# Block-sparse attention and a gated long convolution on one core: keys copied straight into their slots, and later queries split in natural layout and placed by two DMA transposes

## Chip, cores and metric

The kernel runs on one core of a Trainium2 chip. The metric is the device time of one launch in microseconds, as the median of several runs. A separate profiled execution gives the trace; its span goes from its first to its last instruction.

## What is computed

Attention over 4 batches of 8 heads, 768 positions of 64 elements. A query sees its own block of 64 keys and the blocks whose mean key gives one of its three highest gate scores, never a later position. The result is the input of a second stage: a projection to three parts, a circular convolution of one of them along the sequence with a given filter, a product of the three, and an output projection.

```python
def _attn_ref(q, k, v):
    B, H, S, D = q.shape                       # 4, 8, 768, 64
    block, top_k = 64, 3
    k_rep = k.reshape(B, H, n_blocks, block, D).mean(axis=3)
    gate_scores = np.einsum('bhsd,bhnd->bhsn', q, k_rep)
    gate_scores = np.where(causal, gate_scores, -1000000000.0)
    top_idx = np.argsort(gate_scores, axis=-1)[..., -top_k:]
    ...                                        # mask: blocks in top_idx and the own block
    scores = scale * np.matmul(q, k.transpose(0, 1, 3, 2))
    mask = mask & (pos[:, None] >= pos[None, :])
    scores = np.where(mask, scores, -1000000000.0)
    ...                                        # softmax over keys
    return np.matmul(attn, v)

def _moe_ref(x, w_proj, filter_fft, w_out):    # x: heads side by side, 4 x 768 x 512
    proj = x @ w_proj
    x1, x2, x3 = proj[..., :D], proj[..., D:2 * D], proj[..., 2 * D:]
    X2 = np.fft.rfft(x2, n=S, axis=1)
    H = np.fft.rfft(filter_fft, n=S, axis=0)[None, :, :]
    x2_conv = np.fft.irfft(X2 * H, n=S, axis=1)
    return (x1 * x2_conv * x3) @ w_out
```

All inputs and the output are float32.

## The kernel before

**Pairs.** Two heads are worked on together, so there are 16 pairs, four per batch. `prep(g)` brings keys, queries and mask of pair g into the form that the scores need, `attn(g)` computes scores, exponentials and weighted values, and `hyena(b)` does the second stage for a batch once its four pairs are there. `filt()` transforms the filter once, at the start.

**Preparing a pair (`prep`).** Keys of both heads lie side by side in `kn` with the position on the partitions. TensorE transposes them in six float32 blocks (L342), so that a PSUM bank holds head 0 on partitions 0 to 63 and head 1 on 64 to 127. VectorE sums blocks of 64 for the key means (L345), ScalarE casts to float16 into `k2` (L350), and GpSimd splits the means into a high and a low half, `km` (L363, L364). Queries go the same way (L374), but ScalarE scales and casts them into `q2h` (L377) and VectorE writes the rounding error into `q2l` (L380): the gate scores need more than float16 gives. A shuffle then moves each head from its 64 partitions of `k2` or `q2h` to partitions 0 to 63 of the slots `kt` and `qt` (L393 as a DMA from SP; for the first two pairs L395, on VectorE or GpSimd). Twenty small matmuls give the gate scores (L409); VectorE finds the third highest for every query (L422 to L428) and marks the blocks below it in `nm` (L434, L439); five transposes (L450) turn the marks, and two copies (L458) put them on partitions 64 to 75 of `qt`.

**Scores.** Partitions 64 to 75 of `kt` hold a constant, -30720 in the row of the key's block and 0 elsewhere (`eblk`), so that one matmul over 76 partitions (L480) gives score plus mask. ScalarE takes the exponential (L486), GpSimd clears what lies above the diagonal (L491), TensorE multiplies with the values (L508), and VectorE divides (L517, L521) into `xn`. A transposing DMA makes `xT` of it (L540); sums and differences of its halves (L546) go through matmuls with cosines and sines (L558, L565) into `XT`.

**Second stage.** L667 and L676 to L686 multiply in the frequency domain, L703 to L712 project the two other parts and multiply them, L730 transforms back, L761 is the output projection.

**Order.** There is no loop that runs in program order. `build` makes a list of operations, each with the engines that can do it, a cost and a due time `vt` in units of a pair; `plan` simulates five engines (TensorE, ScalarE, VectorE, GpSimd and SP, which issues every DMA), buffers and PSUM banks, takes at each step the operation that can start first, the more urgent first, and so writes out one order for all. `PAR` holds the numbers of the due times, `POOLS` the count of buffers. Each engine then works in that order, and a waiting instruction holds up all behind it on its engine or, on SP, in its queue. Until the planner's `warm_until` TensorE is fed with filler matmuls (L856) where it has nothing else. Operations with `lock` are planned so that VectorE and GpSimd don't overlap.

Of the kernel before, what the change touches and what calls it, by code (L numbers as in the profile page):

```python
# [9 lines left out]
FP32 = mybir.dt.float32  # L10
# [14 lines left out]
KR = D + NB  # L25
# [16 lines left out]
for _pi, _segs in enumerate(PIECES):  # L42
# [6 lines left out]
    p0=-2.579, p1=0.077, a0=0.0, pvlag=0.294, dlag=1.997, dlen=0.945, h0=5.459, hlen=3.658, f0=0.196,  # L49
    f1=4.432, ld=-1.443, s2a=-0.205, s2b=0.422, x0=0.488, x1=0.938, c0=0.578, c1=0.847, o0=1.481,  # L50
    o1=1.0, pen_dve=0.221, ahead=2.229, delta=0.029, queue=6.554, direct=2, late=2.0, w0=1.031, wl=1.656,
    wlag=-0.256, warm_until=30, tr0=-7.197, trl=1.834, fill0=0.703,
)

POOLS = dict(kn=3, qn=3, vn=2, k2=2, q2h=2, q2l=2, ks=2, km=3, m8=2, nm=2,
# [8 lines left out]
class Buf:  # L64
    def __init__(self, pool):
        self.pool, self.slot, self.left = pool, None, 0
        self.w, self.r = {}, {}
        self.free = self.busy = 0.0
        self.users = []
# [7 lines left out]
class Graph:  # L77
    def __init__(self):
        self.ops = []

    def add(self, tag, vt, eng, emit, rd=(), wr=(), res=(), lock=False, size=0):
        o = Op()
        o.i, o.tag, o.vt, o.eng, o.emit, o.lock, o.size = len(self.ops), tag, vt, eng, emit, lock, size
# [25 lines left out]
def pe_cost(mms):  # L109
    occ = sum(mms)  # L110
    return occ, occ - mms[-1] + 0.17 + mms[-1]


def dve(n, rate=1.0):
    occ = n / (960.0 * rate) + 0.066
    return occ, occ + 0.15
# [11 lines left out]
def build(par):  # L128
    g_ = Graph()
# [56 lines left out]
    add("phase", T0, {"DVE": (1.0, 1.15)}, e_phase, wr=[cb("phase"), cb("magic")])  # L186
    add("iota", T0 + .1, {"POOL": pol(1.7)}, e_iota, wr=[cb("cols")])
    add("nyq", T0 + .2, {"DVE": (0.08, 0.23)}, e_nyq, wr=[cb("cols")])
    def e_eblk(E, nc, en):
        nc.gpsimd.memset(E.eblk[64:KR, :], EMASK)  # L190
        nc.gpsimd.affine_select(out=E.eblk[64:KR, :], in_=E.eblk[64:KR, :], compare_op=ALU.is_ge,
                                fill=0.0, base=0, pattern=[[1, S]], channel_multiplier=-64)
        nc.gpsimd.affine_select(out=E.eblk[64:KR, :], in_=E.eblk[64:KR, :], compare_op=ALU.is_ge,
                                fill=0.0, base=63, pattern=[[-1, S]], channel_multiplier=64)

    add("eblk", T0 + 3, {"POOL": pol(2.5)}, e_eblk, wr=[cb("eblk")])


    slot_init = []
    for i in range(POOLS["kt"]):  # L200
        def e_fill(E, nc, en, i=i):
            eng = nc.vector if en == "DVE" else nc.gpsimd
            eng.memset(E.t["qt"][i][64:KR, :, 0:P], 0.0)
            eng.tensor_copy(
                E.t["kt"][i][64:KR, :, :],
# [855 lines left out]
```

## Time and profile before

| | |
|---|---|
| time, median of 3 runs | 249.28 us (249.26 to 249.3) |
| span of the profiled execution | 248.8 us |
| TensorE matmuls, busy | 236.4 us (95%), 2410 of them |
| VectorE, busy | 204.8 us (82%) |
| ScalarE, busy | 175.6 us (71%) |
| GpSimd, busy | 129.3 us (52%) |
| DMA traffic | 40.02 MB, 98945 packets, 89440 of them under 512 B |
| mean granted TensorE clock | 0.991 |

The busy share is a mean over the whole span, in which stages follow one another that have different limits. Matmuls overlap in the record, so TensorE's busy time isn't the time that its work needs; the distance from one start to the next says more. Each digit of the following slices is the busy share of 6.2 us in tenths.

```profile
PE   8978998999889899999999999999999999999994
DVE  7899788988997999998899786778898968589860
ACT  2877999999667679886865796767756873524443
DMA  6999499997999958999976895421415131032006
```

### The profile page before, as it was taken

Reading aid. Unit: us, or ns where it says so; the run is one execution under the profiler, and the core shown is the slowest. Engines: PE = TensorE matmul, PEld = TensorE weight load, DVE = VectorE, ACT = ScalarE, POOL = GpSimd, SP = SyncE. Lnnn points to the kernel's source line nnn. Section 1 sums busy time; section 2 is a strip of 40 time slices with the busy share of each in tenths; the row PEclk is TensorE's granted clock in tenths of the full one; section 3 lists DMA queues with packets and bytes.
Section 4 is the critical chain, followed back from the end, with each engine's and each line's share of the span. In section 5 each row is a group of like instructions: output and inputs, shape, how many; then the busy total and the mean of one; then the engine's idle time right before and its main releaser. Section 6 shows DMA issues by size and latency. Waiting matters only on the chain.

```text
span 248.8 us, 6695 instructions
## 1 busy us (share of the span) xinstructions
PE 236.4 (95%) x2410; PEld 161.1 (65%) x2410; DVE 204.8 (82%) x643; ACT 175.6 (71%) x296; POOL 129.3 (52%) x240
## 2 busy tenths in 40 slices
PE   8978998999889899999999999999999999999994
PEld 6756687678556576867766677677566766645651
DVE  7899788988997999998899786778898968589860
ACT  2877999999667679886865796767756873524443
POOL 6662457675485547554558476643444614063420
PEclk9999999999997999999999999999999999999999
DMA  6999499997999958999976895421415131032006
GB/s 167 336 229 249 102 248 221 233 245 174 275 212 224 234 151 203 247 180 214 216 188 172 195 279 115 107 54 33 108 42 161 42 34 32 9 139 109 3 20 234
DMA packets 98945, 40.02 MB, mean 161 GB/s; under 512 B 89440, under 2 KB 93024, under 8 KB 98912
## 3 DMA queue, kind: packets, MB, share of 16 engines
q1 hardware_dynamic: 98912, 39.60, 66.3%
q8 instruction: 19, 0.31, 0.5%
q14 instruction: 14, 0.11, 0.2%
HBM read 24.64 MB, written 6.29 MB: 124 GB/s over the span
## 4 chain that ended last, share of the span: by engine, by line
PE 79%; DVE 7%; SPq 6%; DMA 3%; ACT 2%; issue 1%; DVEq 0%; ACTq 0%
PE ps L703 16%; PE ps L480 14%; PE ps L761 8%; PE ps L667 8%; PE ps L508 7%; PE ps L730 6%; PE ps L558 4%; SPq L274 3%; PE ps L374 3%; PE ps L342 3%; PE ps L409 2%; PE ps L450 2%; PE ps L565 2%; SPq L297 2%; DMA t<-in_moe_w_out_dram 2%; DVE t L676 2%
## 5 line engine op out<-in xcount | busy, mean ns | idle before, releaser
L486 ACT ACTIVATE ex<-ps 128x1024 f16<-128x1024 f32 (+1 forms) x96 | 86.1, 930 | 14.7 <-PE ps L480 14.4
L491 POOL TENSOR_SCALAR_AFFINE_SELECT ex<-ex 128x256 f16<-128x256 f16 x96 | 41.7, 437 | 52.4 <-ACT ex L486 51.6
L480 PE MATMUL ps<-qt,kt 76*128 76x512 f16 (+3 forms) x256 | 51.2, 310 | 0.3 <-ACT ex L486 0.3
L703 PE MATMUL ps<-xT,wp 128*128 128x384 f16 x256 | 50.5, 326 | 0.0
L703 PEld LDWEIGHTS <-wp 128*128 128x128 f16 x256 | 24.0, 97 | 14.1 <-issue 0.2
L686 POOL TENSOR_TENSOR Y<-t,t 128x512 f16<-128x512 f32 (+1 forms) x18 | 23.4, 1306 | 18.7 <-DVE t L676 18.3
L480 PEld LDWEIGHTS <-kt 76*128 76x128 f16 x256 | 23.1, 99 | 15.1 <-issue 1.4
L508 PEld LDWEIGHTS <-ex 128*128 128x128 f16 x672 | 25.2, 97 | 3.9 <-POOL km L363 0.4
L508 PE MATMUL ps<-va,ex 128*128 128x65 f16 x672 | 26.8, 193 | 0.2 <-DVE nm L434 0.2
L765 ACT COPY osb<-ps 128x512 f32<-128x512 f32 x24 | 14.2, 590 | 15.1 <-PE ps L761 15.0
L667 PE MATMUL ps<-wp,XT 128*128 128x512 f16 x96 | 23.7, 381 | 0.2 <-DVE t L676 0.2
L761 PE MATMUL ps<-wo,yT 128*128 128x512 f16 x96 | 23.8, 379 | 0.0
L751 POOL TENSOR_TENSOR yT<-prod,sd 128x384 f16<-128x384 f32 x16 | 15.9, 1000 | 13.5 <-DVE sd L745 11.2
L712 DVE TENSOR_TENSOR prod<-ps,x 128x384 f32<-128x384 f32 x32 | 17.6, 552 | 6.5 <-PE ps L703 6.2
L350 ACT CAST k<-ps 128x384 f16<-128x384 f32 x32 | 14.7, 481 | 11.3 <-DVE colv L182 4.6
L676 DVE TENSOR_TENSOR t<-ps,HA 128x512 f32<-128x512 f32 x24 | 16.5, 686 | 6.3 <-PE ps L667 6.2
L730 PE MATMUL ps<-G,Y 128*128 128x384 f16 x96 | 20.8, 326 | 0.0
L709 ACT CAST x<-ps 128x384 f16<-128x384 f32 x29 | 14.0, 483 | 9.4 <-PE ps L703 4.6
L345 DVE TENSOR_REDUCE ks<-ps 128x6 f32<-128x384 f32 x32 | 17.1, 552 | 4.1 <-ACT k L350 2.0
L380 DVE SCALAR_TENSOR_TENSOR q2l<-ps,q2h 128x384 f16<-128x384 f32 x32 | 17.0, 551 | 2.3 <-ACT q2h L377 2.2
L521 DVE TENSOR_TENSOR xn<-ps,rec 128x384 f16<-128x384 f32 x32 | 17.8, 556 | 1.0
L745 DVE TENSOR_TENSOR sd<-ce,ps 128x384 f32<-128x384 f32 x32 | 16.3, 549 | 2.2 <-PE ps L730 1.5
(106 smaller groups left out, 435.0 us busy)
## 6 DMA issues: line engine op xcount, KB each, us to landing
kn<-in_k_dram SPq DMA_DIRECT2D x32, 192.0 KB, 3.6
qn<-in_q_dram SPq DMA_DIRECT2D x32, 192.0 KB, 3.6
vn<-in_v_dram SPq DMA_DIRECT2D x16, 384.0 KB, 4.3
out_dram<-osb SPq DMA_DIRECT2D x24, 256.0 KB, 2.0
t<-in_moe_w_proj_dram SPq DMA_DIRECT2D x12, 256.0 KB, 4.2
kt<-k SPq DMA_DIRECT2D x28, 96.0 KB, 3.0
qt<-q2h SPq DMA_DIRECT2D x28, 96.0 KB, 3.5
t<-in_moe_filter_fft_dram SPq DMA_DIRECT2D x6, 256.0 KB, 4.6
```

Of the source, the lines that this page charges most:

```text
L480: nc.tensor.matmul(o[:, col:col + w], lhsT=E.sb(Kt[g])[0:KR, t, P * kc:P * (kc + 1)], rhs=E.sb(Qt[g])[0:KR, t, q0:q0 + w], start=True, sto ...
L486: nc.scalar.activation(E.sb(ex)[:, 0:w], E.sp(sp)[:, 0:w], AF.Exp, scale=ESC)
L491: nc.gpsimd.affine_select(out=dv, in_=dv, compare_op=ALU.is_ge, fill=0.0, base=0, pattern=[[0, 2], [1, P]], channel_multiplier=-1)
L508: nc.tensor.matmul(o[:, 65 * c:65 * c + 65], lhsT=E.sb(exs[pi])[:, col:col + P], rhs=E.sb(va[g])[:, t, kc, :], start=(kc == 0), stop=(kc = ...
L521: nc.vector.tensor_tensor(E.sb(xn)[:, :, t, :], pov[:, :, 0:64], E.sb(rec).rearrange("p (c n) -> p c n", n=1) .to_broadcast([P, NQ, D]), o ...
L667: nc.tensor.matmul(E.bk(xa), lhsT=w, rhs=E.wp[:, j, Dm:2 * Dm], start=(j == 0), stop=(j == NP - 1))
L676: nc.vector.tensor_mul(E.sb(dst), E.bk(xa), m)
L686: (nc.vector if en == "DVE" else nc.gpsimd).tensor_tensor(E.sb(Y)[ro, n_, :], E.sb(x)[ri, :], E.sb(y)[ri, :], op=op)
L703: nc.tensor.matmul(E.bk(xq)[:, 0:HS], lhsT=E.wp[:, d2, 2 * Dm * m + P * dc:2 * Dm * m + P * (dc + 1)], rhs=E.sb(xT[gs[d2]])[:, cs], start= ...
L712: nc.vector.tensor_mul(E.sb(prod)[:, cs], E.bk(xq)[:, 0:HS], E.sb(x1))
L730: nc.tensor.matmul(E.bk(cv)[:, 0:HS], lhsT=E.sb(Y)[:, 3 * p_ + n_, P * dc:P * (dc + 1)], rhs=E.G[:, 3 * p_ + n_, :], start=(n_ == 0), stop ...
L761: nc.tensor.matmul(E.bk(op_), lhsT=E.sb(yT)[:, d2, P * c:P * (c + 1)], rhs=E.wo[:, d2, :], start=(d2 == 0), stop=(d2 == NP - 1))
```

## The change

**Keys.** With the heads on opposite partition halves of a slot, no shuffle is needed for keys. The slots `kt` and `qt` become [128, 6, 2, 128]: for every 128 positions first the columns of head 1, then those of head 0. Head 0 keeps its 64 partitions below and the mask on 64 to 75; head 1 has its data on 64 to 127, the mask on 0 to 11 and zeros between, and its scores are matmuls over 128 partitions. So each half of the key transposes is copied from PSUM into the slot by two instructions of 64 partitions, on ScalarE or VectorE, and the constants of a slot cover more partitions.

**Queries and mask, pairs 0 to 7.** As before, but the shuffle keeps partitions and writes 256 B pieces; the marks are transposed with 128 columns of weights.

**Queries and mask, pairs 8 to 15** (`tm=8`). No TensorE transposes. ScalarE or VectorE scales and casts the queries in natural layout into `qx` in blocks of 128 columns, VectorE writes the rounding error into the blocks between, a transposing DMA (T1, ten blocks of 128 columns) makes the gate's operand `qg` of both. After the gate VectorE writes the marks over the error's place in `qx`, next to the scaled queries, and a second transposing DMA (T2, twelve blocks) writes queries, zeros and mask into `qt` at once.

**Planner.** New values in `PAR`, an offset of the due time and a penalty for VectorE per kind of operation, other costs, slots `kt`, `qt` and `qx` taken in the order of the pairs, and other buffer counts.

```diff
-KR = D + NB
+XW = 2 * P * NQ + 64
+NMW = 64 * NQ
+KR = (76, 128)
...
-    p0=-2.579, p1=0.077, a0=0.0, pvlag=0.294, dlag=1.997, dlen=0.945, h0=5.459, hlen=3.658, f0=0.196,
-    f1=4.432, ld=-1.443, s2a=-0.205, s2b=0.422, x0=0.488, x1=0.938, c0=0.578, c1=0.847, o0=1.481,
-    o1=1.0, pen_dve=0.221, ahead=2.229, delta=0.029, queue=6.554, direct=2, late=2.0, w0=1.031, wl=1.656,
-    wlag=-0.256, warm_until=30, tr0=-7.197, trl=1.834, fill0=0.703,
+    p0=-2.503, p1=0.149, a0=0.0, pvlag=0.364, dlag=1.728, dlen=1.178, h0=5.163, hlen=3.776, f0=-0.278,
+    f1=4.952, ld=-1.045, s2a=-0.184, s2b=0.461, x0=0.517, x1=0.943, c0=0.51, c1=0.761, o0=1.574,
+    o1=1.0, pen_dve=-0.346, ahead=3.319, delta=0.028, queue=6.537, direct=2, tm=8, kin=16, late=2.0,
+    w0=1.334, wl=1.579, wlag=0.085, warm_until=31.758, tr0=-4.639, trl=2.112, fill0=-0.29, v_yT=0.58, v_sd=0.159,
...
-POOLS = dict(kn=3, qn=3, vn=2, k2=2, q2h=2, q2l=2, ks=2, km=3, m8=2, nm=2,
+POOLS = dict(kn=2, qn=3, vn=2, k2=1, qx=4, ks=2, km=3, m8=2, nm=1,
...
+    def e_eblk(E, nc, en, h=0):
+        x = E.eblk[64 * h:64 * h + 64, :]
+        nc.gpsimd.memset(x, EMASK)
...
+    for h in range(2):
+        add("eblk", T0 + 3 + h, {"POOL": pol(2.2)}, lambda E, nc, en, h=h: e_eblk(E, nc, en, h), wr=[(cb("eblk"), h)])
...
-            eng.memset(E.t["qt"][i][64:KR, :, 0:P], 0.0)
-            eng.tensor_copy(
-                E.t["kt"][i][64:KR, :, :],
-                E.eblk[64:KR, :].rearrange("p (o s) -> p o s", o=1).to_broadcast([NB, 2, S]))
...
+            eng.memset(E.t["qt"][i][0:64, :, 0, :], 0.0)
+            eng.memset(E.t["qt"][i][64:76, 0, 1, :], 0.0)
...
+            for h in range(2):
+                r = slice(0, 64) if h == 0 else slice(64, 76)
+                eng.tensor_copy(E.t["kt"][i][r, :, h, :], E.eblk[r, :].rearrange("p (c s) -> p c s", s=P))
...
+                    nc.sync.dma_start(E.sb(dst)[:, :, 1 - t if src == "q" and g >= par["tm"] else t, :],
...
+        direct, by_dma, in_place = g < par["direct"], g >= par["tm"], g < par["kin"]
...
-                    nc.vector.tensor_copy(E.sb(k2)[:, cs], E.bk(kp)[:, 0:HS])
...
             add("kT", v(.0 + .1 * hf), {"PE": pe_cost([0.109] * 3)}, e_kt, rd=[(kn[g], 0), (kn[g], 1), cb("id32")], wr=[kp],
-                res=[k2, ks])
...
+            if in_place:
+                for t in range(2):
+                    def e_k2(E, nc, en, hf=hf, kp=kp, t=t):
+                        r = slice(64 * t, 64 * t + 64)
+                        (nc.scalar.copy if en == "ACT" else nc.vector.tensor_copy)(
+                            E.sb(Kt[g])[r, HC * hf:HC * (hf + 1), 1 - t, :],
+                            E.bk(kp)[r, 0:HS].rearrange("p (c s) -> p c s", s=P))
+                    add("k2", v(.05 + .1 * hf + .02 * t), {"ACT": act(HS), "DVE": dve(HS)} , e_k2, rd=[kp],
+                        wr=[(Kt[g], ("h", t, hf))])
...
+                u = 1 - t if by_dma else t
+                ru = slice(64 * u, 64 * u + 64)
+                cc = slice(12 * u, 12 * u + 12)
+                nc.gpsimd.tensor_copy(x[r, 2, 0:12], E.sb(ks)[r, :])
+                nc.gpsimd.tensor_tensor(x[ru, 1, cc], E.sb(ks)[r, :], x[r, 2, 0:12], op=ALU.subtract)
+                nc.gpsimd.tensor_copy(x[ru, 0, cc], x[r, 2, 0:12])
...
-                    o, i_ = E.sb(dst)[0:64, t, :], E.sb(src)[64 * t:64 * t + 64, :]
+                    r = slice(64 * t, 64 * t + 64)
+                    o = E.sb(dst)[r, :, 1 - t, :]
+                    i_ = E.sb(src)[r, col:col + S].rearrange("p (c s) -> p c s", s=P)
...
+                add(tag, vt, eng, e_sh, rd=[(src, 0), (src, 1)], wr=[(dst, ("h", t, 0)), (dst, ("h", t, 1))],
+                    size=0 if direct else 130, lock=direct)
...
+        if not in_place:
+            shuffle(k2, 0, Kt[g], v(.3), "shK")
...
+        if not by_dma:
+            for hf in range(2):
...
+                    nc.vector.scalar_tensor_tensor(out=E.sb(qx)[:, cl], in0=E.bk(qp)[:, 0:HS], scalar=QS,
...
+            shuffle(qx, 0, Qt[g], v(.4), "shQ")
...
+        else:
+            def blocks(E, first, c0):
+                x = E.sb(qx)
+                return bass.AP(tensor=x.tensor, offset=x.offset + first + 256 * c0, ap=[[XW, P], [256, NQ - c0], [1, P]])
...
+            def e_pq(E, nc, en):
+                eng = nc.vector if en == "DVE" else nc.gpsimd
+                eng.memset(E.sb(qx)[:, 0:64], 0.0)
+                eng.memset(E.sb(qx)[:, 192:320], 0.0)
...
+            def e_qh(E, nc, en):
+                i_ = E.sb(qn[g]).rearrange("p c t d -> p c (t d)")
+                if en == "ACT":
+                    nc.scalar.activation(blocks(E, 64, 0), i_, AF.Copy, bias=0.0, scale=QS)
+                else:
+                    nc.vector.tensor_scalar_mul(blocks(E, 64, 0), i_, QS)
...
+            def e_ql(E, nc, en):
+                nc.vector.scalar_tensor_tensor(out=blocks(E, 192, 1),
+                                               in0=E.sb(qn[g]).rearrange("p c t d -> p c (t d)")[:, 1:NQ], scalar=QS,
+                                               in1=blocks(E, 64, 1), op0=ALU.mult, op1=ALU.subtract)
...
+            def e_T1(E, nc, en):
+                nc.sync.dma_start_transpose(out=E.sb(qg)[:, 0:2 * P * (NQ - 1)].rearrange("p (c s) -> p c s", s=P),
+                                            in_=E.sb(qx)[:, 320:XW])
...
+            def e_T2(E, nc, en):
+                nc.sync.dma_start_transpose(out=E.sb(Qt[g]).rearrange("p c t s -> p (c t) s"),
+                                            in_=E.sb(qx)[:, 0:2 * P * NQ])
...
+            add("pq", v(.0), {"DVE": (0.25, 0.4), "POOL": pol(0.3)}, e_pq, wr=[(qx, "c")], res=[qg], lock=True)
+            add("qh", v(.0), {"ACT": act(S, True), "DVE": dve(S, 2)}, e_qh, rd=[(qn[g], 0), (qn[g], 1)], wr=[(qx, "h")],
+                res=[qg], lock=True)
+            add("ql", v(.05), {"DVE": dve(S - P)}, e_ql, rd=[(qn[g], 0), (qn[g], 1), (qx, "h"), (qx, "c")],
+                wr=[(qx, "l")], lock=True)
+            add("T1", v(.1), {"SP": (1.45, 0)}, e_T1, rd=[(qx, "h"), (qx, "l"), (qx, "m")], wr=[qg], size=510)
+            qs, gin = qg, [qg]
...
-                for n_, (qx, w) in enumerate(((q2h, 0), (q2h, 1), (q2l, 0), (q2l, 1))):
-                    nc.tensor.matmul(o[:, 32 * c:32 * c + 24], lhsT=E.sb(qx)[:, P * c:P * (c + 1)],
+                for n_, (lo, w) in enumerate(((0, 0), (0, 1), (1, 0), (1, 1))):
+                    col = P * (2 * (c - 1) + lo) if by_dma else S * lo + P * c
...
-            n_ = E.sb(nm)
-            nc.vector.tensor_tensor(n_[:, :, :, 0:NB],
+            x = E.sb(qx if by_dma else nm)
+            base, row, cst, tst = (256, XW, 256, 192) if by_dma else (0, NMW, 64, 32)
+            nc.vector.tensor_tensor(bass.AP(tensor=x.tensor, offset=x.offset + base,
+                                            ap=[[row, P], [cst, NQ - 1], [tst, 2], [1, NB]]),
...
+        if by_dma:
+            add("T2", v(.7), {"SP": (1.8, 0)}, e_T2, rd=[(qx, "h"), (qx, "m"), (qx, "c")],
+                wr=[(Qt[g], ("h", t, hf)) for t in range(2) for hf in range(2)] + [(Qt[g], ("m", t)) for t in range(2)],
+                size=612)
+            return
...
-                nc.tensor.transpose(o[0:64, P * c:P * (c + 1)],
-                                    E.sb(nm)[:, c, :, :].rearrange("p t n -> p (t n)"), E.id16)
...
+                nc.tensor.transpose(o[:, P * c:P * (c + 1)], E.sb(nm)[:, 64 * c:64 * c + P], E.id16)
...
-                    E.sb(Qt[g])[64:KR, t, P:S], o[32 * t:32 * t + NB, 0:S - P])
-            add("md", v(.85), {"DVE": (0.398, 0.55), "ACT": (0.59, 0.755)}, e_md, rd=[mt, cb(("slots", g))],
...
+                    E.sb(Qt[g])[r:r + NB, 1:NQ, 1 - t, :],
+                    o[32 * t:32 * t + NB, 0:S - P].rearrange("p (c s) -> p c s", s=P))
+            add("md", v(.85), {"DVE": (0.5, 0.65), "ACT": (0.7, 0.865)}, e_md, rd=[mt, cb(("slots", g))],
                 wr=[(Qt[g], ("m", t))])
...
-                        nc.tensor.matmul(o[:, col:col + w], lhsT=E.sb(Kt[g])[0:KR, t, P * kc:P * (kc + 1)],
-                                         rhs=E.sb(Qt[g])[0:KR, t, q0:q0 + w], start=True, stop=True,
+                        nc.tensor.matmul(o[:, col:col + w], lhsT=E.sb(Kt[g])[0:KR[t], kc, 1 - t, :],
+                                         rhs=E.sb(Qt[g])[0:KR[t], q0 // P:(q0 + w) // P, 1 - t, :],
+                                         start=True, stop=True,
...
+            if b.seq is not None and b.seq > turn[b.pool][0]:
+                return None
...
-                        o.eng, key=lambda x: (at(o, x, f) + o.eng[x][0] + (par["pen_dve"] if x == "DVE" else 0.0), x)):
+                        o.eng, key=lambda x: (at(o, x, f) + o.eng[x][0] + (par.get("d_" + o.tag, par["pen_dve"]) if x == "DVE" else 0.0), x)):
```

## Prediction, made before the changed kernel was seen

> **What bounds the kernel now.** I read the page's busy shares first, then the same by stretches, then single operations.
>
> ```profile
> core 0: us, PE busy (x) PEld busy (x) DVE busy (x) ACT busy (x) POOL busy (x), PEclk, DMA share, GB/s
> 30.00:60.00 30.00, 29.05 (x405) 21.91 (x404) 25.61 (x99) 28.35 (x44) 20.07 (x46) 1.00 0.93 219
> 60.00:95.00 35.00, 31.86 (x364) 21.75 (x362) 30.91 (x114) 26.21 (x45) 19.58 (x38) 0.95 0.97 216
> 95.00:245.00 150.00, 150.00 (x1423) 97.67 (x1419) 122.30 (x337) 99.35 (x169) 73.86 (x125) 1.00 0.51 124
> ```
>
> From 95 to 245 us TensorE is never without work. Its matmuls overlap, so I checked it on start times too: nearly every start follows the one before by the time its own columns need, and the list of waits has no entry for TensorE in that stretch. There the span is the sum of what stands in TensorE's queue. Before 95 us it is different: ScalarE is at 28.35 of 30, then VectorE at 30.91 of 35, the DMA engines over 0.9 throughout, and TensorE pauses. The 3.6 us after 245 are the last eviction and store.
>
> What the change touches on TensorE, once each in the saturated stretch (start, merged duration):
>
> ```profile
> 102.20 0.82 PE L374 MATMUL ps<-id,qn 128*128 128x128 f32 x6
> 102.86 0.81 PE L703 MATMUL ps<-xT,wp 128*128 128x384 f16 x4
> ...
> 123.79 0.47 PE L450 MATMUL ps<-id,nm 128*64 128x128 f16 x5
> 124.19 0.61 PE L480 MATMUL ps<-qt,kt 76*128 76x512 f16 x3
> ```
>
> Durations overlap; what counts is start to next start. The six query transposes of a pair hold TensorE for 102.86 - 102.20 = 0.66 us, the five mask transposes for 124.19 - 123.79 = 0.40 us.
>
> The other rows used below, as mean ns on ScalarE and VectorE (groups by form) and as min/median/max ns of SP's issues (by tile and by line):
>
> ```profile
> L377 ACT ACTIVATE q2h<-ps 128x384 f16<-128x384 f32 x32 | 15.0, 496 | 1.1 <-PE ps L374 1.0
> L350 ACT CAST k<-ps 128x384 f16<-128x384 f32 x32 | 14.7, 481 | 11.3 <-DVE colv L182 4.6 <-PE ps L342 3.3 <-issue 1.7
> L380 DVE SCALAR_TENSOR_TENSOR q2l<-ps,q2h 128x384 f16<-128x384 f32 x32 | 17.0, 551 | 2.3 <-ACT q2h L377 2.2
> L458 DVE COPY qt<-ps 12x640 f16<-12x640 f16 x25 | 12.1, 484 | 2.3 <-PE ps L450 1.8
> ...
> L393 SPq DMA_DIRECT2D kt<-k x28: 461/546/1296, 27.9 to 171.9; - x28
> L393 SPq DMA_DIRECT2D qt<-q2h x28: 467/588/1251, 31.7 to 177.5; - x28
> L540 SPq DMA_TRANSPOSE xT<-xn x16: 1211/1260/3114, 37.4 to 207.5; - x16
> ```
>
> [...] five mask transposes take 0.40 us, and xT, six blocks in one DMA, lands 3.3 us after its issue. [...] the trace shows it after the gaps at 71 to 73 us: six score matmuls then take 1.91 us where they take 1.03.
>
> **The change part by part.**
>
> TensorE, pairs 8 to 15: query and mask transposes go, 0.66 + 0.40 = 1.06 us a pair, 8 pairs, **8.5 us**. They start at 89.0 us (pair 8's queries) and end at 189 us (pair 15's mask), so nearly all lie in the stretch where the queue sets the end. Gate matmuls stay 20 a pair. The second head's scores use 128 rows instead of 76 and mask transposes of pairs 0 to 7 have 128 weight columns instead of 64; the streamed columns are unchanged, so nothing is added. No added instruction runs on TensorE.
>
> Key copies: two of 64x384 instead of one of 128x384 per half, so 2 x 0.481 = 0.96 us more a pair on ScalarE or VectorE. Seven pairs (8 us falls to the rest after 95 us: 7 x 0.96 = 6.7) meet idle time there: ScalarE has 50 us, VectorE 28. Nine pairs' key transposes start before 95 us (4.5 to 86.5), 8.7 us, three in each of 0-30, 30-60 and 60-95. In 30-60 the idle time is 1.65 us on ScalarE and 4.39 on VectorE against 2.9 added; in 60-95 it is 8.8 and 4.1. At least nothing, at most 8.7; I take 1.0 for 30-60, 0.3 for 60-95.
>
> Slot and mask constants, at the start: a second half of eblk, 0.73 + 0.82 + 0.82 = 2.4 us on GpSimd; per slot four writes, which on VectorE I estimate at 1.2 us from the 0.165 and 0.55 us of the two before, over four slots +1.9. VectorE loses the four direct key copies of the first two pairs, 4 x 0.351 = 1.4. The key copies of the first three pairs fall there as well. I take +0.7, bounds -1 and +4. Each pair's key means need two more small GpSimd operations, 0.4 us; GpSimd is idle half of the time, and behind it the gate has its lead.
>
> Query work of pairs 8 to 15: ScalarE loses 2 x 0.496 and gains one of 768 elements (0.496 + 384 x 0.815 ns = 0.81, slope from the two exp forms); VectorE loses 2 x 0.551 and two mask copies of 0.484, gains one of 640 elements, about 0.82, and perhaps 0.3 of zeroing. Per pair with the keys: ScalarE +0.8, VectorE -1.0. Over 95-245 that is 99 to 106 and 122 to 115 us of some 141: neither becomes the bound.
>
> SP's queue: 28 key shuffles go (15.3 us), and 16 query shuffles (9.4). Each later pair issues two transposes of 10 and 12 blocks; at xT's 1.26 us for six, 2.1 + 2.5 = 4.6 us, or at least 2 x 1.26 if issue doesn't grow with blocks. Net per later pair between +0.3 and +2.4 us, at most 19 in all; summing its issue durations, SP issues for 56.8 of the 105 us from 95 to 200, so it fits on average. It is a queue in order: the first transpose waits there for ScalarE's and VectorE's split, the second for the mask, and key, query and value loads, xT and stores of other pairs stand behind them.
>
> DMA engines: the two transposes move 0.33 and 0.39 MB[...]. The packet records give 0.38 us of all 16 engines for a shuffle, so 4 x 0.38 goes per later pair[...]. Earlier, twelve key shuffles go (4.5 us) and twelve query shuffles get 256 B pieces instead of 1536 B (+1.3). That relieves the stretch at 0.93 to 0.97, and scores no longer wait for a key landing (median 3.0 us): I take -1.2, bounds 0 and -3.5.
>
> Latency of a later pair's queries: split 0.8 + 0.8, first transpose about 4.1 to landing (2.1 issue, then xT's 2.0), gate 0.5, mask on VectorE 1.9, second transpose 4.5: 12.7 us. In the trace a pair's query transposes lead its first scores by 14.5 us (pair 8), 17 (pair 9), 20 to 29 later. It fits, with least room for pair 8, whose queries are issued at 77 us. I take no wait.
>
> The planner's numbers (PAR, costs, the rule that slots are taken in pair order) reorder all engines, and kn, nm and k2 have one buffer less. The trace can't show the new order. In the saturated stretch an order that keeps TensorE fed is worth nothing more; before 95 us it can win back at most the 12 us of pauses between 30 and 95 (summed from start times against each form's usual interval) or lose as much as the key copies. kn's third buffer is hidden by loads that land 10 us and more ahead of their transposes (76 against 86.5 us for pair 8); I take 0, bounds -3 and +4.
>
> Sum: 249.28 - 8.5 + 1.0 + 0.3 + 0.7 - 1.2 = 241.6; I say **241.5**. The profiled span is 248.8 and the timed runs 249.26 to 249.3, so differences are carried over to 249.28 as they are.
>
> **Rivals.**
> - The early stretch gains: fewer DMAs where they are saturated; those 12 us of pauses leave room. Three to four us more, 238. Against it: the chain of waits there is VectorE's (30% of 60-72 us in one line, L676), which gets no relief.
> - The key copies cost their full 8.7 us before 95 us, which would just cancel the gain. Half of it, with the bounds of the start, gives 245.5. For it: ScalarE at 28.35 of 30.
> - Slower: the two transposes in SP's queue. If landing, waiting behind one another and behind loads (4.6 us of issue more than I count) exceeds the lead, 12.7 + 4.6 - 14.5 = 2.8 us of TensorE pause per pair[...]. Above 1.06 us a pair over eight pairs the gain is gone; with 2.8 us in half of the pairs, 249.3 - 8.5 + 11.2 = 252. Against it: the later leads of 20 us and more.
> - The transposes stay on TensorE: excluded by the diff, which returns before them for pair 8 onwards.
>
> **How the numbers follow.** My forecast (239.5 to 244) 0.53; early gain (235 to 239.5) 0.17; key copies (244 to 248.7) 0.18; the same within 0.2% (0.5 us, about what a measurement of this kernel can tell from no change) 0.02; slower 0.10. So faster 0.88. The range 237.5 to 247.5 leaves out the slower and equal cases, a third of the early gain and the worst of the key copies: about 0.2.
>
> **What would show it.** Right: TensorE's matmul count lower by 88, still 150-odd us without a pause to its end, its last matmul some 8 us sooner; ScalarE's key copies twice as many at about 0.48 us; xT-like DMAs 16 more, landing in 3 to 6 us. Wrong: TensorE waits on the second transpose or on the gate in 100 to 200 us; a saturated stretch that begins later than 95 us by more than 2 us; or SP's issue of a transpose far from 2 us.

## The result and the profile after

The changed kernel takes **246.73 us** (246.44 to 246.96, four runs) against 249.29 us: a ratio of 0.990 [0.988, 0.991]. The forecast was 241.5, with a range of 237.5 to 247.5. The direction is right and the time lies near the slow end of the range, but the gain is 2.6 us where 7.8 were forecast. In the table of the experiments, the medians leave out one run of queries_only and two of shuf4_pool (granted clocks 0.979, 0.993 and 0.986), which took over 1.5% longer than the fastest run of the same kernel.

Of the two traces' difference, 248.8 - 245.2 = 3.6 us, some 1.2 us don't belong to the change: the profiled execution of the kernel before took 250.48 us, 1.2 more than its median, with a stretch at half clock near 75 us (granted clock 0.50 from 74 to 77 us; the prediction's six score matmuls of 1.91 us start there, at 75.17). And the trace of the kernel after is of the slowest of its four runs (246.96).

The page of the kernel after, from parts 1 and 4 (busy time by engine; the chain that ended last, by engine):

```profile
PE 229.1 (93%) x2330; PEld 154.4 (63%) x2330; DVE 207.7 (85%) x642; ACT 171.5 (70%) x287; POOL 151.2 (62%) x304
PE 57%; ACT 18%; DVE 16%; issue 5%; POOL 3%; DVEq 0%; ACTq 0%; POOLq 0%
```

TensorE has 80 matmuls fewer: the 88 transposes less, eight fillers more. In the kernel before 79% of the chain was TensorE's; now ScalarE and VectorE carry a third of it.

The same stretches as before (columns as in the prediction's first fence; the last now ends at 242), and 95 to 150 us by itself:

```profile
30.00:60.00 30.00, 27.26 (x381) 20.29 (x380) 24.45 (x99) 27.38 (x45) 20.51 (x50) 1.00 0.85 206
60.00:95.00 35.00, 33.07 (x384) 23.02 (x383) 30.37 (x106) 31.08 (x50) 25.62 (x56) 1.00 0.93 218
95.00:242.00 147.00, 142.16 (x1335) 90.19 (x1333) 128.32 (x350) 90.89 (x151) 82.84 (x152) 1.00 0.62 139
95.00:150.00 55.00, 50.96 (x499) 33.22 (x498) 49.32 (x144) 39.52 (x69) 39.02 (x78) 1.00 1.02 213
```

The kernel before in the last of these stretches:

```profile
95.00:150.00 55.00, 55.00 (x614) 38.70 (x611) 49.02 (x156) 43.36 (x72) 33.66 (x66) 1.00 0.92 214
```

TensorE was full there; now it lacks 4 of 55 us and starts 115 matmuls fewer in the same time. Yet no compute engine is full: ScalarE is even less busy than before, VectorE about as busy. The DMA share is above 0.9 in both kernels. I count as a pause of TensorE what a start comes later than the median distance after a matmul of the same width and type (the texts on record count a little differently). By that count its pauses between 95 and 200 us grow from 3.1 to 7.9 us, nearly all of it before 150 (1.7 and 6.8). Before 30 us they are 7.5 and then 6.9, from 30 to 95 us 10.9 and then 9.5; the half-clock stretch is in the 10.9.

One such pause, of 1.2 us, ends at 116.07. First the matmuls ahead of it, then the chain of waits that leads to it (start, duration, what):

```profile
114.04 1.03 PE L849 MATMUL ps<-wo,yT 128*128 128x512 f16 x4
```

```profile
113.20 0.38 ACT XT L659
113.58 0.36 ACT kt L381
...
113.95 0.47 ACT kt L381
...
114.45 0.47 ACT kt L381
...
114.94 0.21 ACT kt L381
115.15 0.29 issue
115.44 0.59 ACT osb L853
116.03 0.04 issue
116.07 1.02 PE ps L849 x4
```

The output projection (L849) waits for a PSUM bank. The eviction `osb` that frees it stands on ScalarE behind four key copies (L381), which run one after another for 1.95 us, from 113.47 to 115.42; `osb` follows at 115.44. That ScalarE is idle at other times doesn't help the eviction.

Not all of this pause is the copies' doing. The four matmuls that fill the bank end at 115.07 and `osb` starts at 115.44, so it was held up by 0.37 us; the rest is the eviction itself, for which the next product waits as well. TensorE's waits for `osb`, in the kernel after and in half_keys, which leaves two of the four copies out:

```profile
PE ps L849 <- ACT osb L853: 1.0, 1, 1.0
PE ps L851 <- ACT osb L855: 0.7, 1, 0.7
```

So the pause shows the mechanism, but the copies' share in it is small. Matmul by matmul, half_keys shortens some twenty of TensorE's pauses by 0.2 to 0.5 us each; there is no long one.

What the prediction priced, in the kernel after: the copies and the split (groups by form), and SP's two transposes (ns, min/median/max):

```profile
L381 ACT CAST kt<-ps 64x384 f16<-64x384 f32 x59 | 27.9, 473 | 11.5 <-DVE ks L371 6.4 <-PE ps L368 4.6
L463 DVE SCALAR_TENSOR_TENSOR qx<-qn,qx 128x640 f16<-128x640 f32 x8 | 7.3, 908 | 0.0
L458 ACT ACTIVATE qx<-qn 128x768 f16<-128x768 f32 x8 | 6.8, 852 | 0.0
```

```profile
L468 SPq DMA_TRANSPOSE qx<-qx x8: 1352/2003/2820, 93.7 to 171.8; - x8
L472 SPq DMA_TRANSPOSE qt<-qx x8: 1302/1418/2345, 110.2 to 183.7; - x8
```

The single prices hold: 0.473 us a copy of 64 partitions (0.481 used, the time of one of 128), 0.85 and 0.91 for the split (0.81 and 0.82), 2.0 us for the first transpose's issue (2.1). The second issues in 1.4, where 2.5 was used. TensorE's list of waits has no entry for either transpose.

### The profile page after: what moved, and what is told of

The parts are those of the page before. It is cut to its first block, busy times and chain, and to the rows that moved or that the text cites. A ratio compares the mean times of both kernels' runs of the same rounds, so it can differ in the third digit from the quotient of the medians.

```text
span 245.2 us, 6521 instructions
## 1 busy us (share of the span) xinstructions
PE 229.1 (93%) x2330; PEld 154.4 (63%) x2330; DVE 207.7 (85%) x642; ACT 171.5 (70%) x287; POOL 151.2 (62%) x304
## 2 busy tenths in 40 slices
DMA packets 122304, 41.45 MB, mean 169 GB/s; under 512 B 116384, under 2 KB 116384, under 8 KB 122272
## 3 DMA queue, kind: packets, MB, share of 16 engines
q1 hardware_dynamic: 122272, 41.04, 72.2%
## 4 chain that ended last, share of the span: by engine, by line
PE 57%; ACT 18%; DVE 16%; issue 5%; POOL 3%; DVEq 0%; ACTq 0%; POOLq 0%
PE ps L791 12%; PE ps L566 8%; ACT ex L573 8%; PE ps L755 8%; PE ps L849 7%; ACT kt L381 7%; PE ps L950 5%; PE ps L596 4%; PE ps L818 4%; DVE ks L371 4%; PE ps L646 2%; DVE prod L800 2%; PE ps L368 2%; PE ps L488 2%; DVE sd L833 1%
## 5 line engine op out<-in xcount | busy, mean ns | idle before, releaser
L573 ACT ACTIVATE ex<-ps 128x1024 f16<-128x1024 f32 (+1 forms) x96 | 85.1, 930 | 14.5 <-PE ps L566 14.0
L578 POOL TENSOR_SCALAR_AFFINE_SELECT ex<-ex 128x256 f16<-128x256 f16 x96 | 42.3, 448 | 33.2 <-ACT ex L573 32.4
L566 PE MATMUL ps<-qt,kt 76*128 76x512 f16 (+7 forms) x256 | 48.7, 305 | 2.8 <-ACT ex L573 1.9
L791 PE MATMUL ps<-xT,wp 128*128 128x384 f16 x256 | 48.8, 326 | 0.6 <-DVE t L764 0.3
L381 ACT CAST kt<-ps 64x384 f16<-64x384 f32 x59 | 27.9, 473 | 11.5 <-DVE ks L371 6.4
L774 POOL TENSOR_TENSOR Y<-t,t 128x512 f16<-128x512 f32 (+1 forms) x22 | 27.8, 1269 | 12.9 <-DVE t L764 12.6
L566 PEld LDWEIGHTS <-kt 76*128 76x128 f16 (+1 forms) x256 | 22.9, 97 | 20.1 <-issue 5.2
L849 PE MATMUL ps<-wo,yT 128*128 128x512 f16 x96 | 23.7, 379 | 1.0 <-ACT osb L853 1.0
L371 DVE TENSOR_REDUCE ks<-ps 128x6 f32<-128x384 f32 x32 | 16.8, 550 | 5.5 <-ACT kt L381 4.8
L839 POOL TENSOR_TENSOR yT<-prod,sd 128x384 f16<-128x384 f32 x10 | 10.4, 1051 | 15.4 <-DVE prod L800 13.0
L950 PE MATMUL ps<-warm 128*128 128x256 f16 x114 | 17.2, 299 | 1.1 <-DVE warm L170 1.1
L634 POOL TENSOR_TENSOR eo<-xn 128x384 f16<-128x384 f16 x18 | 17.2, 957 | 1.1 <-DVE xn L609 0.7
L659 ACT CAST XT<-ps 128x512 f16<-128x512 f32 (+1 forms) x22 | 11.0, 511 | 9.8 <-PE ps L653 5.7
```

The costliest lines, as they stand in the source:

```text
L371: nc.vector.reduce_sum(E.sb(ks)[:, 6 * hf:6 * hf + 6], E.bk(kp)[:, 0:HS].rearrange("p (n t) -> p n t", t=64), axis=AX.X)
L381: (nc.scalar.copy if en == "ACT" else nc.vector.tensor_copy)(E.sb(Kt[g])[r, HC * hf:HC * (hf + 1), 1 - t, :], E.bk(kp)[r, 0:HS].rearrange( ...
L566: nc.tensor.matmul(o[:, col:col + w], lhsT=E.sb(Kt[g])[0:KR[t], kc, 1 - t, :], rhs=E.sb(Qt[g])[0:KR[t], q0 // P:(q0 + w) // P, 1 - t, :], ...
L573: nc.scalar.activation(E.sb(ex)[:, 0:w], E.sp(sp)[:, 0:w], AF.Exp, scale=ESC)
L578: nc.gpsimd.affine_select(out=dv, in_=dv, compare_op=ALU.is_ge, fill=0.0, base=0, pattern=[[0, 2], [1, P]], channel_multiplier=-1)
L774: (nc.vector if en == "DVE" else nc.gpsimd).tensor_tensor(E.sb(Y)[ro, n_, :], E.sb(x)[ri, :], E.sb(y)[ri, :], op=op)
```

## The experiments

Theory: the error is in the key copies, which cost time in ScalarE's queue although ScalarE has idle time. Rivals: turns of two engines at the copies' PSUM bank; the transposing DMAs and SP's queue; TensorE's own term; the planner's new numbers. All times are medians, with the difference to the kernel after:

| kernel | us | ratio to before, 95% | to after |
|---|---|---|---|
| before_again | 249.25 | [0.999, 1.001] | +2.5 |
| keys_only | 252.23 | [1.009, 1.013] | +5.5 |
| queries_only | 247.47 | [0.988, 0.996] | +0.7 |
| neither | 249.59 | [1.001, 1.004] | +2.9 |
| no_T | 246.57 | [0.986, 0.992] | -0.2 |
| half_keys | 241.01 | [0.964, 0.969] | -5.7 |
| half_4to7 | 243.59 | [0.976, 0.979] | -3.1 |
| half_8up | 243.71 | [0.976, 0.979] | -3.0 |
| key_time_no_bank | 246.39 | [0.984, 0.990] | -0.3 |
| key_bank_no_time | 242.86 | [0.971, 0.976] | -3.9 |
| twice_after | 248.99 | [0.997, 0.999] | +2.3 |
| twice_half | 243.77 | [0.976, 0.979] | -3.0 |
| qh_pool | 255.46 | [1.018, 1.029] | +8.7 |
| shuf4 | 247.56 | [0.988, 0.995] | +0.8 |
| shuf4_pool | 250.65 | [1.003, 1.009] | +3.9 |
| shuf8_pool | 253.59 | [1.012, 1.020] | +6.9 |
| shuf12 | 245.67 | [0.984, 0.987] | -1.1 |

**The kernel before once more** (before_again), for the noise between runs.

> The kernel before, unchanged, for a second trace. The trace shown before the prediction came from an execution of 250.48 us, 1.2 above the median of 249.28, with TensorE at half clock around 72 to 78 us. If that stretch was the execution's own, a second trace has a span near 247.6, no half-clock stretch and its pauses before 95 us are shorter by about 1.5 us; then 1.2 us of what the sum seemed to lose was never there. If the half clock belongs to the kernel, the span is again 248.8.

The traced execution, of 251.95 us, has a stretch at a lower clock as well (mean granted clock 0.90 in 60 to 95 us), so there is no trace of an undisturbed one. But 17 of the 19 runs lie between 249.21 and 249.28 us, so the 1.2 us of the first trace belong to its execution.

**The parts by themselves**, each planned anew with the changed kernel's numbers: `tm=16` (keys_only), `kin=0` (queries_only), both (neither); `k2=2` where keys are shuffled.

```diff
-    o1=1.0, pen_dve=-0.346, ahead=3.319, delta=0.028, queue=6.537, direct=2, tm=8, kin=16, late=2.0,
+    o1=1.0, pen_dve=-0.346, ahead=3.319, delta=0.028, queue=6.537, direct=2, tm=16, kin=0, late=2.0,
```

> The changed kernel with tm=16: all pairs keep their query and mask transposes on TensorE, keys are copied in place; planned anew with the changed kernel's numbers. If the keys' part is what costs (A), it is slower than the kernel before by 2 to 5 us: 251.5 to 254, since nothing pays for the copies. If the queries' part costs (B), it is no slower than before: 248 to 250. In either case at most 8.5 us above the changed kernel.

> The changed kernel with kin=0 and two k2 buffers: keys are cast once into k2 and moved by SP's shuffles as in the kernel before (in the new slot layout, in pieces of 256 B), queries and mask of pairs 8 to 15 by the transposing DMAs; planned anew with the changed kernel's numbers. If the two parts add up, the queries' part is worth what the changed kernel has over keys alone, 252.2 - 246.7 = 5.5 us, and up to the 8.5 us of TensorE's queue: 241 to 244, faster than both kernels. If the gain needs the keys' part (SP's queue or the DMA engines can't carry shuffles and transposes together): 247 or more.

> The changed kernel with tm=16 and kin=0: all queries, masks and keys as in the kernel before, but in the new slot layout and planned with the new numbers. Theory A: near the kernel before, 248.5 to 250.5. Theory C, the new numbers and the new order cost something by themselves: 251 or more.

Neither part: 0.3 us slower than before, so layout and numbers together are worth about nothing in that version. Keys alone cost 2.9 us. Queries alone bring 1.8 us (four runs between 246.49 and 248.63), far from the 241 to 244 that I expected, so the parts don't add up: alone they come to a loss of 1.1 us, together they gain 2.6. Why is open. With shuffles and transposes queries_only loads the DMA engines more (133472 packets against 122272 after, 81% of 16 engines over the span against 72%), but between 95 and 200 us TensorE's list of waits there has no DMA. It has GpSimd's masking (L578, 1.5 us) and VectorE's L634 (1.3) on top, and its order is another. The next sets keep the changed kernel's order and edit only what an operation emits.

**No transposing DMAs** (no_T).

```diff
             def e_T1(E, nc, en):
+                return
...
             def e_T2(E, nc, en):
+                return
```

> The changed kernel in its own order, without the sixteen transposing DMAs of pairs 8 to 15 (gate and scores read what the buffers held before). Takes away their issue on SP, their traffic and every wait for them, and nothing else. Theory B, their latency and SP's queue cost the gain: 3 us or more less, 243.5 or lower. Theories A and C: within 0.7 us of the changed kernel, 246 to 247.

The stretch from 95 to 150 us in no_T:

```profile
95.00:150.00 55.00, 50.98 (x500) 33.24 (x498) 49.32 (x145) 39.52 (x69) 39.17 (x79) 1.00 0.70 166
```

No gain beyond the noise: the transposes, their issue and their latency cost nothing here. This refutes the slower rival. It also excludes that the transposes' load on the DMA engines makes the pauses: the DMA share falls from 1.02 to 0.70, and TensorE starts 500 matmuls where it started 499.

**Key copies left out** (half_keys from the fifth pair on; half_4to7 and half_8up divide that in two).

```diff
                     def e_k2(E, nc, en, hf=hf, kp=kp, t=t):
+                        if g >= 4 and t == 1:
+                            return
```

> The changed kernel in its own order, but from pair 4 on the second head's two key copies are left out (its slot keeps the keys of four pairs earlier), 24 copies of 0.47 us less, nearly all on ScalarE. Theory A, the doubled key copies hold up evictions and exponentials behind them on ScalarE: the pauses of TensorE between 95 and 150 us shrink from about 6.6 us to under 3.5 and the time falls by 3 to 5 us, to 242 to 244. Theory B, the pauses come from the transposing DMAs: under 1 us, 246. Theory C, the pauses come from VectorE's load and the new order: under 1.5 us.

> The complement: the copies of the second head's keys are left out for the fifth to eighth pair alone (8 copies, 3.8 us), between 40 and 77 us. Theory 1: all of the 5.7 us comes back here, 241 to 241.7. Theory 2, both stretches alike: 1.9 us, 244.4 to 245.2. Theory 3: nothing here, 246.2 to 247. If both parts give more together than 5.7, a pause removed early is given back later or the reverse.

> The order of after; the copies of the second head's keys are left out from the ninth pair on alone (16 copies, 7.6 us of ScalarE and VectorE), so those heads' scores use what the slot held. With the copies left out from the fifth pair on (24) the time was 241.0. Theory 1, the prediction's own step (copies after 95 us meet idle time, only the earlier ones cost): within 0.7 us of after, 246 to 247.2. Theory 2, the copies cost in both stretches alike, about half of their ScalarE time: 16 of 24 of 5.7 us, so 242.4 to 243.4. Theory 3, all of the loss lies after 95 us, as the pauses there rose from 2.3 to 6.6 us: 241 to 241.8.

24 copies cost 5.7 us, more than the 3 to 5 that I expected; the pauses between 95 and 150 us fall from 6.8 to 4.4, less than expected. The copies cost in both parts: eight between 41 and 74 us cost 3.1, 0.83 of their 3.8 us of engine time; sixteen between 83 and 170 us cost 3.0, 0.40 of their 7.6. Neither half's time lies in one of the three ranges that I expected for it. Together the two halves give 6.1, so only 0.4 us is counted twice. Since the order is the same, each matmul's start can be compared in the two traces: by that half_keys gains 3.3 us from 30 to 95 us of the kernel after and 2.2 behind it, 1.6 of these by 120. Neither half of the prediction's step holds. The first four pairs' copies fill slots that hold nothing yet; leaving those out was not tried.

**Time or bank.** key_time_no_bank lets the second copy read a constant in SBUF: same engine time (22 of them on ScalarE, 0.508 us each), no PSUM bank. key_bank_no_time copies 24 elements instead of 384, with every wait and the bank as in the kernel after. The second head's slots are therefore wrong or partial in both.

```diff
+                        src = E.colv[r, 0:HS] if g >= 4 and t == 1 else E.bk(kp)[r, 0:HS]
...
-                            E.bk(kp)[r, 0:HS].rearrange("p (c s) -> p c s", s=P))
+                            E.sb(Kt[g])[r, HC * hf:HC * (hf + 1), 1 - t, :], src.rearrange("p (c s) -> p c s", s=P))
```

```diff
+                        n = 8 if g >= 4 and t == 1 else P
...
-                            E.sb(Kt[g])[r, HC * hf:HC * (hf + 1), 1 - t, :],
-                            E.bk(kp)[r, 0:HS].rearrange("p (c s) -> p c s", s=P))
+                            E.sb(Kt[g])[r, HC * hf:HC * (hf + 1), 1 - t, 0:n],
+                            E.bk(kp)[r, 0:HS].rearrange("p (c s) -> p c s", s=P)[:, :, 0:n])
```

> The changed kernel in its own order, but from pair 4 on the second head's two key copies read a constant row in SBUF instead of the PSUM bank of the transposes, at about the same duration (384 elements of 64 partitions). ScalarE works as long as in the changed kernel; the bank is shared by one copy and the sum instead of two and the sum. Theory A1, ScalarE's time in its queue costs the 5.7 us that leaving the copies out brought: 246 to 247. Theory A2, the bank, held by three readers one after the other, costs them: 241 to 242.5.

> The changed kernel in its own order, but from pair 4 on the second head's two key copies take 24 elements of a partition instead of 384 (about 0.2 us instead of 0.47), from the same bank with the same waits. Theory A1 (ScalarE's time): 24 x 0.27 = 6.5 us less work and most of the 5.7 us back, 241.5 to 243.5. Theory A2 (turns at the bank, not time): less than half of it back, 244 to 246.5.

The short copies in key_bank_no_time (groups by form):

```profile
L382 ACT CAST kt<-ps 64x384 f16<-64x384 f32 x37 | 17.5, 472 | 10.0 <-PE ps L368 5.0 <-DVE ks L371 4.7
L382 ACT CAST kt<-ps 64x24 f16<-64x24 f32 x22 | 3.8, 174 | 2.3 <-DVE ks L371 2.0
```

Without the bank but with the time nothing changes beyond the noise (-0.3 us); with the bank but without most of the time 3.9 of the 5.7 us come back. The short ones still take 0.174 us of 0.473, so 63% of the copies' time is gone and 68% of their cost. It is the engine's time, roughly in proportion. The waits between L371 and L381 on that bank, the longest of the copies' own in the profile after (6.4 us), are not the price.

**What TensorE's work is worth now.** The later pairs' key transposes done twice, in the kernel after (twice_after) and without the copies of half_keys (twice_half).

```diff
-                for c in range(HC):
+                for c in (range(HC) if g < 8 else 2 * list(range(HC))):
```

> After, with the six key transposes of each pair from the ninth on done twice (same bank, same result): 48 more transposes of 0.109 us start to start, 5.2 us of TensorE between 86 and 166 us and nothing else. It asks what TensorE's work is worth in the changed kernel. Theory that TensorE's queue still sets the time: 251.5 to 252. Theory that ScalarE's queue sets it between 95 and 150 us and TensorE's pauses take up a part: 249 to 251. None of it is felt (under 247.5): then the 8.5 us that the transposes on TensorE were priced at was never to be had either.

> The same doubling of the later pairs' key transposes in the version without the second head's key copies from the fifth pair on (those heads' scores use what the slot held), which took 241.0. There TensorE should be the one that sets the time: 5.2 us more by its queue alone, 245.8 to 246.4. Under 244.5 would say that TensorE's work is not what sets the time even there, and that the gain of the left-out transposes was mis-sized as well.

5.2 us more of TensorE is felt as 2.3 us in the kernel after, and as 2.8 even without the copies; I had expected 4.8 to 5.4 there, and that missed. The rest goes into pauses: by start times TensorE's pauses over the whole span fall by 2.8 and 2.3 us, and 2.3 + 2.8 and 2.8 + 2.3 give nearly the 5.2 back. So TensorE's own term was not all to be had either once its queue no longer sets the pace alone.

**Can ScalarE be relieved?** qh_pool moves the later pairs' query scaling to GpSimd.

```diff
-                    nc.scalar.activation(blocks(E, 64, 0), i_, AF.Copy, bias=0.0, scale=QS)
+                    nc.gpsimd.tensor_scalar_mul(blocks(E, 64, 0), i_, QS)
```

> The order of after; the scaling of the later pairs' queries (128x768, 0.85 us on ScalarE, eight of them) goes to GpSimd at the same place of the program. That takes 6.8 us off ScalarE and leaves every key copy where it is. Theory 1, ScalarE's time is what the key copies cost: 24 left-out copies gave back 5.7 us for 11.4 us of ScalarE, so 6.8 us give 2 to 3.5, 243.2 to 244.7. Theory 2, only the key copies' own place in the chain from key transposes to scores counts, not ScalarE's time in general: within 0.5 us of after, 246.2 to 247.2. Theory 3, GpSimd is too slow for it and the first transposing DMA comes late: over 247.5.

The moved operation in qh_pool, by line:

```profile
L458 POOL TENSOR_SCALAR qx<-qn x8: 2124/2134/2565, 85.2 to 175.3; 128x768 f16<-128x768 f32 x8
```

8.7 us slower (6.6 in the fastest run). ScalarE falls from 39.52 to 33.03 us in 95 to 150, but GpSimd goes from 39.02 to 46.31 and the operation takes 2.13 us instead of 0.85. VectorE's part of the split waits for it (3.3 us in all), and TensorE now waits for GpSimd's masking of the exponentials (2.6) and for L774 (2.0), which don't stand in its list in the kernel after. On GpSimd it needs 2134 / 768 = 2.8 ns a column, 2.2 times GpSimd's own 128x768 select of the values (0.95 us in the kernel after, same types, though not in blocks of 128 columns). The test says nothing against the theory of ScalarE's time, since it moves the queueing to an engine that takes 2.13 us where ScalarE takes 0.85; it does show again that free time on an engine, here GpSimd's 16 of 55 us, wasn't room.

**Shuffles instead of the second copy**: one 128x384 copy a half into `k2` (three buffers) and two DMAs a pair, from the fifth pair (shuf4), with the scaling on GpSimd (shuf4_pool; shuf8_pool from the ninth), and from the 13th pair (shuf12).

```diff
+                        if g >= 4:
+                            x = E.t["k2"][g % 3]
...
+                            if t == 0:
+                                (nc.scalar.copy if en == "ACT" else nc.vector.tensor_copy)(
+                                    x[:, HS * hf:HS * (hf + 1)], E.bk(kp)[:, 0:HS])
+                            if n == 4:
+                                for u in range(2):
+                                    ru = slice(64 * u, 64 * u + 64)
+                                    nc.sync.dma_start(E.sb(Kt[g])[ru, :, 1 - u, :],
+                                                      x[ru, :].rearrange("p (c s) -> p c s", s=P))
+                            return
```

> The order of after, but from the fifth pair on a half's keys leave PSUM in one 128x384 copy into a buffer of their own and two shuffling DMAs a pair bring them to the slot, as in the kernel before; the queries stay as in after. Theory 1, ScalarE's time: as with the left-out copies of the second head, 241 to 243. Theory 2, what held up the version with shuffled keys and transposed queries (248.2) was the load on DMA engines and SP's queue, not its order of work: 246 or more, with DMA share near 0.9 after 95 us and TensorE waiting on key landings.

> Both edits: shuffled keys from the fifth pair on, and the later pairs' query scaling on GpSimd. Theory 1, ScalarE's time: some 0.5 to 1.5 us below the version with the shuffles alone, since ScalarE is then no longer the bound, 240 to 242. Theory 2, DMA and SP's queue hold it: as the version with the shuffles alone, 246 or more.

> Shuffled keys only from the ninth pair on (8 pairs, 16 shuffles instead of 24), where DMA share is lowest, and the later pairs' query scaling on GpSimd. Theory 1, ScalarE's time: key copies of the fifth to eighth pair stay, 8 x 0.473 = 3.8 us more of ScalarE than with shuffles from the fifth on, about 1.9 us: 242 to 244. Theory 2, DMA and SP's queue before 95 us hold up the shuffles: this one is faster than the version with shuffles from the fifth pair on, by over 1 us.

> The order of after; shuffled keys (one copy a half, two DMAs a pair) from the 13th pair on alone, 8 shuffles where the DMA share first falls, from 130 us. Frees 3.8 us of ScalarE. Theory of ScalarE's time with DMA able to carry it: 244.5 to 245.5, faster than after. Theory that the DMA engines (share above 1.0 until 155 us) are what made shuffles from the fifth pair on (247.6) no faster: 246.5 or more, with key landings above 3 us and TensorE waiting on loads.

TensorE's list of waits in shuf4 (us in total, times, longest):

```profile
PE ps L578 <- DMA qt<-qx: 3.0, 2, 2.0
PE ps L368 <- DMA kn<-in_k_dram: 2.6, 3, 1.4
```

and its stretch from 95 to 150 us:

```profile
95.00:150.00 55.00, 48.21 (x482) 31.52 (x483) 46.92 (x142) 32.70 (x56) 37.62 (x75) 1.00 1.07 217
```

shuf4 has as few key copies as half_keys (40 instead of 64; ScalarE is busy 32.70 us in this stretch), and is no faster than the kernel after: its four runs lie between 246.27 and 249.16 us, and the trace is of the slowest. TensorE now waits for queries from the second transpose and for key loads, neither of which stood in that list before; it doesn't wait for the shuffled keys. Two things can be seen. SP is busy issuing: the tenth pair's key loads are issued at 87.0 and 91.5 us instead of 82.2 and 86.0, while the median landing of key loads is no longer than before (3.4 and 3.7 us). And the second transposes land later, in a median of 4.6 us instead of 3.7. So it is the DMA path that keeps shuffles and transposes from being had together here; how much of it is SP's queue, in an order planned without shuffles, and how much the DMA engines, isn't separated. Both versions with the scaling on GpSimd repeat qh_pool's loss, so that their theories can't be told apart. shuf12 puts only eight shuffles in, from 129 us, where fewer loads remain: 245.67 us, between the two ranges that I expected, 1.1 us faster than the kernel after, and **the fastest here that leaves nothing out** (its interval [0.984, 0.987] and that of after, [0.988, 0.991], don't touch).

## Why the prediction missed its size

- **The step that failed: the key copies.** "Seven pairs ... meet idle time there: ScalarE has 50 us, VectorE 28", hence nothing after 95 us, and 1.3 us before it. The runs show 5.7 us for the second head's copies from the fifth pair on: by start times 3.3 us up to 95 us, where 1.3 was forecast, and 2.2 after it, where nothing was. The 4.4 us between 5.7 and 1.3 are most of the 5.2 by which the forecast was too fast; without those copies the kernel takes 241.0. The second rival (key copies, 244 to 248.7) comes nearest to what happened, but the copies cost half of their engine time (5.7 of 11.4 us), not all of it, and not only before 95 us.
- **Why idle time didn't hide them.** I compared an engine's busy time with the stretch. What counts is where the copies, up to four in a row, stand in ScalarE's order, and who waits for what is behind them: `osb`, which started 0.37 us after its matmuls' end, and the exponentials, and through them TensorE. In 95 to 150 us ScalarE is idle for 15.5 us and its work still sets pauses. And the 50 us of idle time were those of 150 us, while the copies come between 97 and 170.
- **TensorE, 8.5 us.** The instructions went as counted, and the wider ones add nothing: from start to start a score matmul of 512 columns takes a median of 0.215 us over 128 partitions and 0.219 over 76 (in the trace after), a mask transpose 0.056 us with 128 columns of weights (after) as with 64 (before). But the list took TensorE's saving as felt in full. Between 95 and 200 us 4.8 us came back as pauses (3.1 to 7.9); with the second copies gone 5.1 are left, 2.0 more than before. Added TensorE work is felt by only 43 to 53%. That half_keys comes out near the forecast means that the other terms were right in their sum, not one by one, and that is luck.
- **The start (+0.7) and DMA relief (-1.2).** TensorE's pauses before 30 us don't grow. From 30 to 95 us they are 6.9 in half_keys against 10.9 before, of which 1.2 was that execution's own: a relief of 2.8 us where 1.2 was taken. DMA share does fall from 0.93 to 0.85 and from 0.97 to 0.93 before 95 us; but later it rises, from 0.92 to 1.02 in 95 to 150 us, and packets from 98912 to 122272. By the packet records (72.2% of 245.2 us after, 57.7% of 244.8 in no_T) the two transposes of a pair take 4.5 us of all 16 engines, where four shuffles of the kernel before take 4 x 0.38 = 1.5. Neither term was tested alone, so whether the relief is the DMA engines' or the new order's is open.
- **SP's queue, the slower rival.** Refuted by no_T, and by the absence of waits on either transpose in the profile after. The estimate of 4.6 us of issue a pair was high by 1.2. SP's queue does work in order, as two issues of the kernel before show: it stands for 4.2 us at a key shuffle that awaits ScalarE's copy (L350), and an `xT` whose data was complete at 87.36 us is issued behind that shuffle, at 90.55.
- **The planner's numbers**, taken as nothing: 0.3 us slower in neither, together with the new layout; what the order does in the changed kernel isn't measured.
- **The signs named in advance.** The 88 transposes are gone (80 matmuls in all), the copies' duration came as forecast, and the landing in 3 to 6 us (3.2 to 5.8) too. The one for "wrong" that came true is the saturated stretch that begins late: 150 rather than 95 us. The last matmul starts 3.7 us sooner between the two traces, not 8.

Still open: what the copies of the first four pairs cost, and what makes the early relief, which makes up for the part of TensorE's 8.5 us that is not felt.

## What to carry to other kernels

Added work on an engine that isn't full was not free here: 11.4 us of copies, nearly all on a ScalarE that is busy for 70% of the span, cost 5.7, since TensorE awaited what stood behind them. Price such work by looking, in the chain, at what stands behind it. When work is taken off the bound engine, ask at once what the next pace is: of 5.2 us of TensorE work, 2.3 to 2.8 were felt. And two changes that use the same queues, as the keys' and the queries' part do here, must be tried together, because alone they can show another sum (a loss of 1.1 us instead of a gain of 2.6).

## What the runs showed of the hardware

- A copy from PSUM to float16 on ScalarE takes 0.473 us for 64x384 and 0.481 us for 128x384 (the latter in the kernel before), so half the partitions save next to nothing; one of 64x24 still takes 0.174 us.
- Transposing DMAs within SBUF, in the kernel after: of ten 128x128 blocks, a median of 3.9 us (3.4 to 5.8) from issue to landing and 2.0 us of SP's time; of twelve, 3.7 us (3.2 to 4.5) and 1.4 us of SP's time. The larger one needs less.
- A scaling with cast from float32 to float16 of 128x768 takes 2.13 us on GpSimd, 0.85 on ScalarE.
